# Decay attention and gated convolution: pinning two engines instead of five to the written order of steps

## The chip, the cores and the metric

The kernel runs on one core of a Trainium2 chip. The core has five engines that run side by side: TensorE (PE in the profile; its weight loads are a row of their own, PEld), VectorE (DVE), ScalarE (ACT), GpSimd (POOL) and SyncE (SP). Each engine takes the instructions of its own queue in order, and semaphores hold an instruction back until what it needs from another engine is there. SP does no arithmetic here; it only issues transfers, and so does POOL for some of them. Sixteen DMA engines move the data.

The metric is device time in microseconds, median of several runs. Lower is better.

## What is computed

All arrays are float32. For each of 4 x 8 heads (768 steps, 48 channels) a state decays by a complex factor and takes in the outer product of key and value; the query reads its real part. The heads are then laid side by side (384 channels), and a gated convolution with two projections follows.

```python
for t in range(S):
    ar, ai = (a_re_n[:, :, t, :, None], a_im_n[:, :, t, :, None])   # a, with its magnitude held under 0.999
    new_re = ar * S_re - ai * S_im
    new_im = ar * S_im + ai * S_re
    kv = np.einsum('bhd,bhe->bhde', k[:, :, t], v[:, :, t])
    S_re, S_im = (new_re + kv, new_im)
    y[:, :, t] = np.einsum('bhd,bhde->bhe', q[:, :, t], S_re)
...
x = y.transpose(0, 2, 1, 3).reshape(B, S, H * D)
gate = 1.0 / (1.0 + np.exp(-gate_pre))      # gate_pre: causal convolution of x, 5 taps per channel
val = x @ w_val
out = (gate * val) @ w_out
```

## The kernel before

The 32 heads are cut into ten units (line 76): two of two heads, six of four, two of two. A unit goes through these stages.

- **Loads.** `load` (line 109) brings `ar`, `ai`, `k` and `q` of a unit into one of six slots of the pool `ld` (tag "in"), each array by two transfers on SP (line 114). `load_v` (line 125) brings the values into a pool of three slots (line 132). A slot is free again when the last instruction that reads it is done.
- **Preparation.** `prep_x`, `prep_r`, `prep_a`, `prep_s` and `prep_e` (lines 269 to 367) turn the decay into logarithm and angle, sum both over time (ACT and DVE in turns, with the small matrix products of `offset` on PE), and give cosine, sine and two exponentials. The first step of a unit is the logarithm of `ar` on ACT (line 278); the product with `ai` on DVE (line 284) follows, then the square on ACT (line 289).
- **Scaling.** `prep_b` (line 369) multiplies keys and queries in (line 379, then line 382 into `kx`, of which there is one slot, and into `trig`). `kx` is written to a tensor in device memory, `kd`, by two transfers on SP (line 392).
- **Reading back.** `load_kn` (line 402) reads `kd` back, laid out by chunks of 128 steps, into one of three slots `kn`, for half a unit at a time. The first instruction of a slot is a small memset on POOL (line 407), then come three transfers on SP (line 413: one for the first half of the heads, two for the second, whose rows are swapped in halves).
- **Attention.** `transpose` (line 416) turns `kx` and the scaled queries by PE, and ACT copies them out (lines 430 and 431). For every chunk of a unit (60 in all) PE makes scores (lines 457, 458), DVE masks them into `sm` (line 464), PE makes the output from `sm` and from the state so far (lines 477, 480), ACT copies it (line 481), and PE and ACT carry the state on (lines 494 to 497).
- **Collecting.** `collect` (line 499) moves the attention's output into `xT`, channels on partitions, by transfers on POOL (line 509); `xT`'s first columns are zeroed by a memset on POOL (line 503).
- **Convolution and projection.** `conv` (line 515) is one multiplication (line 518) and four multiply-adds (line 521) on DVE for each group of channels. `gate` (line 527) is the sigmoid on ACT. `project` (line 531) makes the two matrix products on PE (line 255, tiles `pv` and `po`), the product with the gate on DVE (line 542), and the copy on ACT (line 576). The result leaves by transfers on POOL (line 813).
- **Weights.** `load_weights` (line 212) brings the weights in and converts them by short DVE and ACT instructions (lines 186 to 208).

What sets the order: `ORDER` (line 22) is a string with one letter per step, written out by hand, and the loop at line 850 takes it letter by letter. Capital `L`, `V` and `N` are the loads of lines 109, 125 and 402, `D` is `collect`, `O` an output transfer; `X x R r A a S E B` are the preparation, `T` is `transpose`, `s k t y` are scores, mask, state and output of a chunk, `C`, `G` and `M` convolution, gate and projection, `W` the weights. Between two steps the program checks (lines 605 to 834) that a step isn't written before what it builds on; these checks decide when a letter may stand, they are no waits of the chip.

The program text is then handed to a scheduler, which puts the instructions of each engine into a queue. It goes through the program in a timeline of its own: an engine that is idle there takes, of its instructions whose inputs and whose slot are ready, the one that was written first. Slots are given out in the same pass: an instruction that opens a tile takes whichever slot of its pool is free then. After that each queue is fixed, and the chip executes it in that order.

Before, the lines 855 to 865 take this freedom away. They go through all instructions and tie each one of an engine named in `IN_ORDER` to the one before it on the same engine. The tie is used for ordering alone; it makes no wait on the chip.

```python
before = {}
for ins in nc.cur_bb.bb.instructions:
    if ins.engine not in IN_ORDER:
        continue
    if ins.engine in before:
        tc.add_manual_dep(
            ins, before[ins.engine].name,
            mybir.DependencyInfo(mybir.DependencyClass.NoSync, mybir.DependencyReason.DATA),
            reason="the order that the steps are written in",
        )
    before[ins.engine] = ins
```

Of the kernel before, what the change touches and what calls it, by code (L numbers as in the profile page):

```python
# [32 lines left out]
    "MDMOOMMMMMOCCCCCCGMMMMMMMMOOMMO"  # L33
)
IN_ORDER = (
    mybir.EngineType.PE, mybir.EngineType.Activation, mybir.EngineType.DVE, mybir.EngineType.SP, mybir.EngineType.Pool
)
TURN = 2.0 ** 24
RADIAN = 2.0 * PI / 2.0 ** 32 * (1.0 - 2.0 ** -22)
# [962 lines left out]
```

## Time and profile before

| what | value |
| --- | --- |
| median of 3 runs | 351.83 us (351.12 to 354.74) |
| the profiled execution, whole | 351.17 us |
| its span, first to last instruction | 349.4 us |
| mean granted TensorE clock | 0.924 |
| ACT table loads (line 104), 31 of them | 39.8 us busy |
| moved by DMA | 53.31 MB, mean 153 GB/s |

The table's times are read in this way. The span is what the trace covers; the execution is 1.8 us longer than it. Busy time says how long an engine worked, and the rest of its span is waiting: the view of the waits lists, for each engine, which instruction waited, for what, how long in total, how often, and the longest single case. A row "SPq" there is the queue of the engine that issues transfers: while its head waits, everything behind it in the queue waits too. The timeline lists instructions with start and length; what stands in brackets at the end of a row is the idle time just before it and what ended that.

### The profile page before, as it was taken

The page shows a single profiled execution, that of the slowest core. Times are in us where ns is not written, and L with a number is a line of the kernel's source. Part 1 is how long each engine was busy: PE and PEld are TensorE (multiplying, and loading weights), DVE is VectorE, ACT ScalarE, POOL GpSimd, SP SyncE. Part 2 cuts the span into 40 slices and gives each one's busy share as a digit, 9 for nine tenths or more (in the row PEclk, how much of TensorE's full clock was granted, in tenths as well). Part 3 has the DMA queues.
Part 4 walks back from the last instruction along what each step waited for, and adds up shares of the span by engine and source line. Part 5 has one row for each costly group of instructions (what it writes and reads, how often), then busy time and mean ns, then how long its engine had stood idle before and what let it go on. Part 6 is the DMA issues. An engine that isn't in the chain of part 4 may idle for free.

```text
span 349.4 us, 8122 instructions
## 1 busy us (share of the span) xinstructions
PE 269.5 (77%) x3234; PEld 210.8 (60%) x3234; DVE 257.9 (74%) x341; ACT 245.7 (70%) x455; POOL 60.1 (17%) x148
## 2 busy tenths in 40 slices
PE   0033757668977999996669999979989999999960
PEld 0023646538866777576458787668779666766530
DVE  4799869995959999929297899577769956476400
ACT  5758789999657899987357989956996457553110
POOL 3000001111023032020212022200342031240210
PEclk9999887956989999999968999996999999999995
DMA  7993576768697851595969403768950441530220
GB/s 203 316 224 112 140 231 182 108 207 221 172 239 200 167 169 48 193 272 170 258 127 208 108 33 102 218 176 259 191 139 26 124 105 46 154 93 2 85 68 7
DMA packets 87804, 53.31 MB, mean 153 GB/s; under 512 B 36432, under 2 KB 84816, under 8 KB 87760
## 3 DMA queue, kind: packets, MB, share of 16 engines
q1 hardware_dynamic: 83664, 43.28, 48.8%
q0 software_dynamic: 4096, 9.44, 9.1%
q8 instruction: 27, 0.44, 0.5%
q14 instruction: 17, 0.14, 0.1%
HBM read 33.83 MB, written 14.16 MB: 137 GB/s over the span
## 4 chain that ended last, share of the span: by engine, by line
DMA 24%; DVE 19%; PE 18%; ACT 16%; issue 9%; SPq 8%; POOL 2%; POOLq 0%; DVEq 0%; ACTq 0%
DMA kn<-kd 14%; SPq L114 4%; ACT L104 4%; PE pt L430 3%; PE pv L255 3%; PE po L255 3%; ACT kq L431 3%; DVE sm L464 3%; DVE z L521 2%; DMA kd<-kx 2%; DVE kx L382 2%; DVE main L379 2%; DMA raw<-in_moe_w_val_dram 2%; SPq L413 2%; PE sc_ps L457 2%
## 5 line engine op out<-in xcount | busy, mean ns | idle before, releaser
L509 POOL DMA_DIRECT2D xT<-y_sb x80 | 40.8, 516 | 156.3 <-ACT y_sb L481 120.8
L431 ACT COPY kq<-pt 96x384 f32<-96x384 f32 x128 | 51.8, 508 | 4.4 <-PE pt L430 4.2
L521 DVE SCALAR_TENSOR_TENSOR z<-xT,cw_sb,z 128x768 f32<-128x768 f32 (+1 forms) x60 | 51.4, 856 | 1.7
L480 PE MATMUL y_ps<-sm,v_in 128*48 128x128 f32 x384 | 44.0, 294 | 10.2 <-DVE sm L464 10.2
L255 PE MATMUL po<-wo_sb,z 128*64 128x384 f32 x288 | 51.2, 488 | 0.0
L255 PE MATMUL pv<-xT,wv_sb 128*64 128x384 f32 x288 | 49.8, 486 | 0.0
L464 DVE TENSOR_TENSOR sm<-sc_ps,mask 128x512 f32<-128x512 f32 (+1 forms) x60 | 34.5, 578 | 15.9 <-PE sc_ps L458 11.8
L430 PE MATMUL pt<-ident,kx 128*96 128x128 f32 x192 | 37.9, 314 | 9.8 <-DVE kx L382 9.5
L457 PE MATMUL sc_ps<-kq 96*64 96x128 f32 x384 | 43.2, 286 | 1.7 <-DVE sm L464 1.7
L477 PE MATMUL y_ps<-kq,S_sb 96*48 96x128 f32 x320 | 38.5, 300 | 7.3 <-ACT y_sb L481 5.1
L458 PE MATMUL sc_ps<-kq 96*64 96x64 f32 x384 | 43.3, 229 | 0.0
L458 PEld LDWEIGHTS sc_ps<-kq 96*64 96x64 f32 x384 | 40.1, 143 | 2.0
L104 ACT ACT_TABLE_LOAD x31 | 39.8, 1283 | 1.3 <-PEq L986 0.8
L430 PE MATMUL pt<-ident,trig 128*96 128x128 f32 x192 | 36.7, 306 | 4.7 <-DVE trig L382 2.8
L457 PEld LDWEIGHTS sc_ps<-kq 96*64 96x64 f32 x384 | 33.6, 145 | 4.6 <-DVE sm L464 2.1
L255 PEld LDWEIGHTS pv<-xT,wv_sb 128*64 128x64 f32 x288 | 25.8, 137 | 16.1
L494 PE MATMUL S_ps<-v_in,kn 128*64 128x48 f32 x320 | 30.0, 233 | 7.2 <-ACT S_sb L497 5.1
L480 PEld LDWEIGHTS y_ps<-sm,v_in 128*48 128x48 f32 x384 | 28.6, 133 | 11.2 <-DVE sm L464 11.2
L481 ACT COPY y_sb<-y_ps 112x256 f32<-112x256 f32 (+1 forms) x60 | 19.5, 324 | 21.9 <-PE y_ps L480 21.6
L255 PEld LDWEIGHTS po<-wo_sb,z 128*64 128x64 f32 x288 | 24.6, 136 | 15.4 <-DVE z L542 1.5
L430 PEld LDWEIGHTS pt<-ident,kx 128*96 128x96 f32 x192 | 24.1, 144 | 14.4 <-issue 11.9
L477 PEld LDWEIGHTS y_ps<-kq,S_sb 96*48 96x48 f32 x320 | 22.6, 132 | 15.6 <-ACT y_sb L481 8.1
(84 smaller groups left out, 487.6 us busy)
## 6 DMA issues: line engine op xcount, KB each, us to landing
kd<-kx SPq DMA_DIRECT2D x12, 576.0 KB, 4.4
out_dram<-ot POOLq DMA_DIRECT2D x24, 192.0 KB, 2.5
ar_in<-in_a_re_dram SPq DMA_DIRECT2D x12, 288.0 KB, 4.5
ai_in<-in_a_im_dram SPq DMA_DIRECT2D x12, 288.0 KB, 5.2
k_in<-in_k_dram SPq DMA_DIRECT2D x12, 288.0 KB, 4.4
q_in<-in_q_dram SPq DMA_DIRECT2D x12, 288.0 KB, 4.4
xT<-y_sb POOLq DMA_DIRECT2D x48, 72.0 KB, 3.2
v_in<-in_v_dram SPq DMA_DIRECT2D x16, 144.0 KB, 5.1
```

What stands on the lines that cost most here:

```text
L104: nc.scalar.preload_act_table_set(name)
L255: nc.tensor.matmul(out[c:c + 64], lhsT[:, c:c + 64], rhs, **kw)
L430: nc.tensor.transpose(pt[:C2, j, :], src[:, j, f, h, :], ident)
L431: nc.scalar.copy(tj[:, s, f], pt[:C2].rearrange("c j p -> c p j"))
L457: nc.tensor.matmul(sc[lo:lo + half, h, :], k[:, :half], q, start=True, stop=True)
L458: nc.tensor.matmul(sc[hi:hi + half, h, half:], k[:, half:], q[:, half:], start=True, stop=True)
L464: nc.vector.tensor_tensor(out=two(sm), in0=two(sc[:, :g]), in1=mask[:, :, None, :].to_broadcast([C, 2, g // 2, C]), op=ALU.mult)
L477: nc.tensor.matmul(o, self.S_sb[n - 1][:, h * D:(h + 1) * D], self.part(1, h, n), start=True, stop=False)
L480: nc.tensor.matmul(o, vt[:, h, n], sm[:, h, :], start=(n == 0), stop=True)
L494: nc.tensor.matmul(S_all[:64, cols], kn[:, c0:c0 + 64], vt[:, h, n], **at_h)
L509: XQ.dma_start(out=xTs[b][c0 % P:c0 % P + c2 - c0, c0 // P, EXT + hf * HS:EXT + (hf + 1) * HS], in_=self.y[hf][r0:r0 + c2 - c0, h // 2],)
L521: nc.vector.scalar_tensor_tensor(out=z, in0=xT[:, c, EXT + t0 - t:EXT + t0 - t + n], scalar=cw_sb[:, TAPS - 1 - t, c:c + 1], in1=z, op0=AL ...
```

## The change

`IN_ORDER` names TensorE and ScalarE alone. The ties of lines 855 to 865 are made for these two as before; VectorE, SyncE and GpSimd get none, so that the scheduler orders their queues. The string of steps, the instructions themselves, the pools and their slots stay as they are.

```diff
@@ -33,7 +33,7 @@
     "MDMOOMMMMMOCCCCCCGMMMMMMMMOOMMO"
 )
 IN_ORDER = (
-    mybir.EngineType.PE, mybir.EngineType.Activation, mybir.EngineType.DVE, mybir.EngineType.SP, mybir.EngineType.Pool
+    mybir.EngineType.PE, mybir.EngineType.Activation
 )
 TURN = 2.0 ** 24
 RADIAN = 2.0 * PI / 2.0 ** 32 * (1.0 - 2.0 ** -22)
```

## The prediction

> **What bounds the kernel now.** I read the page's busy times first, then the waits of each engine, then the timeline of SP's queue against those of DVE and ACT.
>
> ```profile
> span 349.4 us, 8122 instructions
> PE 269.5 (77%) x3234; PEld 210.8 (60%) x3234; DVE 257.9 (74%) x341; ACT 245.7 (70%) x455; POOL 60.1 (17%) x148
> ```
>
> No engine is full. Three of them are near 250 us, so the span is made of work on PE, DVE and ACT and of stalls in which one holds up the others. The waits say what the stalls are.
>
> ```profile
> DVE main L284 <- DMA ai_in<-in_a_im_dram: 21.4, 5, 6.3
> DVE sm L464 <- PE sc_ps L458: 11.8, 6, 4.0
> DVE z L518 <- DMA xT<-y_sb: 8.2, 2, 5.0
> DVE sm L464 <- PE y_ps L480: 4.1, 3, 3.5
> ACT main L278 <- DMA ar_in<-in_a_re_dram: 13.1, 6, 4.5
> ACT tmp L289 <- DVE main L284: 8.2, 3, 6.0
> PE y_ps L480 <- DVE sm L464: 10.2, 6, 4.9
> PE pt L430 <- DVE kx L382: 9.5, 1, 9.5
> ```
>
> The largest wait of DVE is for the load of `ai`, and ACT's for a transfer is the load of `ar`. These loads are late because SP's queue is held up, which its own waits show:
>
> ```profile
> SPq L413 <- DMA kn<-kd: 70.3, 20, 6.9
> SPq L392 <- DVE kx L382: 44.0, 3, 23.6
> ```
>
> Each of the 20 reads of `kn` issues one transfer and then holds the queue until it has landed, 3.5 us on average; and a write of `kd` stands at the head of the queue until DVE has made `kx`. Loads behind them wait, although nothing they need is missing. Here is SP's queue, with the start of each entry:
>
> ```profile
> 122.16 1.00 SPq L114 DMA_DIRECT2D ar_in<-in_a_re_dram  x2
> 140.85 1.23 SPq L392 DMA_DIRECT2D kd<-kx  x2
> ...
> 148.63 1.22 SPq L114 DMA_DIRECT2D ai_in<-in_a_im_dram  x2
> ...
> 165.20 2.72 SPq L114 DMA_DIRECT2D ai_in<-in_a_im_dram  x2
> ...
> 191.75 1.03 SPq L114 DMA_DIRECT2D ar_in<-in_a_re_dram  x2
> ...
> 224.18 1.10 SPq L114 DMA_DIRECT2D ai_in<-in_a_im_dram  x2
> ...
> 233.22 0.92 SPq L114 DMA_DIRECT2D ar_in<-in_a_re_dram  x2
> ```
>
> and here DVE, with the idle time before an instruction in brackets:
>
> ```profile
> 109.32 1.35 DVE L284 TENSOR_TENSOR main<-tmp,ai_in 128x1152 f32<-128x1152 f32 x1
> ...
> 154.62 1.36 DVE L284 TENSOR_TENSOR main<-tmp,ai_in 128x1152 f32<-128x1152 f32 x1 [6.34 <-DMA ai_in<-in_a_im_dram]
> ...
> 174.28 1.36 DVE L284 TENSOR_TENSOR main<-tmp,ai_in 128x1152 f32<-128x1152 f32 x1 [6.02 <-DMA ai_in<-in_a_im_dram]
> 175.56 0.69 DVE L464 TENSOR_TENSOR sm<-sc_ps,mask 128x512 f32<-128x512 f32 x1
> ...
> 212.48 1.35 DVE L379 TENSOR_TENSOR main<-main,k_in 128x1152 f32<-128x1152 f32 x1
> ...
> 229.42 0.76 DVE L284 TENSOR_TENSOR main<-tmp,ai_in 128x576 f32<-128x576 f32 x1 [5.87 <-DMA ai_in<-in_a_im_dram]
> ```
>
> In the first of these stalls SP did nothing from 123.2 to 140.85 but wait for `kx`, with the load of unit 6's `ai` behind it.
>
> **What the change does to SP.** A load needs a free slot and nothing else. The row at 191.75 is the first load of unit 8, made while `k` of unit 6 (read at 212.48) still held its slot, so any free slot serves. Counting the loads of units 0 to 9 in their order against six slots, `ai` of a unit finds a slot once `ai` of the unit before and `k` and `q` of three units before are read. Unit 6's could go when 109.32 + 1.35 = 110.7 is past, and it went at 148.63; unit 7's could go at 156.0 (154.62 + 1.36) and went at 165.20; unit 8's could go at 175.6 (174.28 + 1.36) and went at 224.18. A load takes about 5 us:
>
> ```profile
> ai_in<-in_a_im_dram SPq DMA_DIRECT2D x12, 288.0 KB, 5.2
> ```
>
> so each would be there before DVE comes for it (148.3, 168.3 and 223.5, the starts less the idle times). A scheduler that issues what is ready will put these loads into the gaps of the `kn` reads, and these waits go. SP's other steps (values, `kd`, `kn`, 60 transfers of line 413 and 20 of line 392) are only passed by loads; what they lose is an issue of 0.6 us here and there, and the second and third transfers of a `kn` read wait for the first to land anyway.
>
> **What of it counts.** An idle DVE costs time only where another engine stands with it. In the last of the five rows below PE worked half of its time and ACT a third: DVE waits for `ai` of unit 7, `sm` of 175.56 stands behind it, PE waits 4.9 us for that `sm`, ACT waits 5.96.
>
> ```profile
> 221.70 0.67 ACT L278 ACTIVATE main<-ar_in 128x576 f32<-128x576 f32 x1
> 175.68 1.16 ACT L289 ACTIVATE tmp<-main 128x1152 f32<-128x1152 f32 x1 [5.96 <-DVE main L284]
> 236.59 0.68 ACT L278 ACTIVATE main<-ar_in 128x576 f32<-128x576 f32 x1 [4.53 <-DMA ar_in<-in_a_re_dram]
> 230.00:240.00 10.00, 7.20 (x98) 6.43 (x96) 9.91 (x10) 4.07 (x11) 0.00 (x0) 0.75 0.74 219
> 170.00:180.00 10.00, 5.12 (x33) 3.76 (x29) 5.68 (x6) 3.33 (x6) 0.51 (x2) 0.68 0.68 168
> ```
>
> I take 4.9 us for this stall, the least of the three waits. For the stall at 229 and 236 I take ACT's 4.5: unit 9's `ar` could go once unit 8's logarithm has read its own (221.70 + 0.67 = 222.4; by the count above `k` and `q` of unit 6 are read by then too), and went at 233.22; DVE was full just then (9.91 of 10) because 5.87 us of waiting had pushed its work there. The stall at 154 reached ACT with 1.7 (8.2 less 6.0 leaves 2.2 for two cases, and 0.6 of it lies in the next rows). In the early part ACT waits
>
> ```profile
> ACT main L278 <- DMA ar_in<-in_a_re_dram: 3.0, 2, 2.1
> ACT main L278 <- DMA ar_in<-in_a_re_dram: 1.6, 1, 1.6
> ACT tmp L289 <- DVE main L284: 0.6, 1, 0.6
> ACT main L278 <- DMA ar_in<-in_a_re_dram: 3.4, 1, 3.4
> ```
>
> (the first row from 0 to 30, the next two from 30 to 60, the last from 60 to 100). The first 3.0 are the kernel's start and stay; the others are 5.6 us. DVE is nearly full there, so I count half, 2.8. Together 4.9 + 4.5 + 1.7 + 2.8 = 13.9 us. The bounds: nothing, if PE is late next everywhere; and 21.4, DVE's whole wait.
>
> The granted clock of the 170 to 180 row is 0.68. The Trainium skill (page "TensorE: Matmul & The Clock Gate", Part 1) says that an idle window of about 3.4 us puts TensorE's clock to half until it has been busy for as long again; the row agrees in kind, and by that rule each of three stalls gone would give some 1.7 us more, an estimate, for a sum near 336.
>
> **What the change does to DVE.** Its 341 instructions stay; where the scheduler sees DVE idle, it takes a later step early. A step in progress can't be broken off, so an urgent `sm` that comes meanwhile waits for the rest of it. That can happen where DVE now idles ahead of `sm`, 6 + 3 times by the waits; half a mean DVE instruction is 257.9 / 341 / 2 = 0.38 us, together 3.4 us lost. Against it stand PE's 9.5 us for one `kx` and the 5.3 us for `sm` not counted yet (10.2 less 4.9): between 14.8 gained and, by the convolution rival below, some 20 lost. I take the 3.4 lost, since most of DVE's time is full and the order hardly free there.
>
> **What it does to POOL.** Its memsets, 80 collecting transfers and 24 output transfers may pass each other.
>
> ```profile
> POOL xT L509 <- ACT y_sb L481: 120.8, 16, 18.3
> POOL kn L407 <- PE S_ps L494: 2.0, 1, 2.0
> ```
>
> POOL mostly waits for ACT, whose order stays, so I cost this at nothing. The cover is the 17% load; if it is gone, a collecting step of five transfers waits behind an output transfer, half a microsecond each.
>
> **Sum.** The profiled execution is 351.17 us, its span 349.4; the median 351.83 is 0.7 above. 351.17 - 13.9 + 3.4 = 340.7, so **341 us**, 3% faster.
>
> **Rivals.**
>
> *The convolution's heads block DVE (slower).* The queue is fixed by the scheduler's own estimate of when data comes, and the chip can't pass a head that is not ready. The Trainium skill (page "PSUM — Partial Sum Buffer", section "Engine vs sequencer instructions") calls the queues of VectorE and GpSimd strict FIFO; the `sm` of 175.56 behind its late neighbour agrees. The place is line 518, 15 starts, each after transfers of `xT`. Pulled forward while DVE seems idle, such a start stands at the head until its transfer lands:
>
> ```profile
> xT<-y_sb POOLq DMA_DIRECT2D x48, 72.0 KB, 3.2
> ```
>
> Now two starts wait, 8.2 us, 4.1 each, with masks and preparation behind. It decides from three more starts on (10.5 / 4.1 = 2.6). With five it gives 340.7 + 5 x 4.1 = 361 us. For it: two such waits exist even in the written order. Against it: a start that is ready in the written order is ready at the same place still.
>
> *Earlier loads delay the reads of kn (no change).* DMA engines are busy 0.68 to 0.74 of the time in the two windows above. The slowest `kn` transfers show what a full system does; a queue wait was 3.5 us on average and 6.9 at the most. If 3 of the 20 reads come 3.4 us later with PE waiting, 10 us are lost, and the time is 351. Against it: the bytes stay the same, and loads would leave a busy place as often as they enter one.
>
> *PE is late next, or the scheduler's order is the written one (no change).* In its own timeline the stalls may not exist, and then the tie removes nothing: 351. Against it: the queue of SP holds loads back for reasons that any timeline sees.
>
> **Chances.** The forecast 0.49; DVE's reordering gaining as well (329 to 335) 0.05; no change, by the two rivals together, 0.16; slower 0.30. A measurement of this kernel tells about 1% from no change, so faster by more than that 0.54, within 0.16, slower 0.30. The forecast's own range is 334 to 347. The whole range starts at 330, with DVE's 14.8 partly got beside the loads, and ends at 362, with five blocked starts; 0.2 lies outside, most of it above.
>
> **What would show it.** SP's queue has loads of line 114 inside the groups of line 413, and unit 6's `ai` goes before 125. The waits of line 284 for `ai` and of line 278 for `ar` fall under 5 us each (3.0 of the latter are the start of the kernel). ACT's wait at line 289 is near 0. Wrong is the prediction if DVE's waits for `xT` at line 518 or PE's for `sm` grow by 10 us, if SP's wait for `kx` holds up `kn` instead, or if the waits for `ai` stay.

## The result

The changed kernel takes 341.53 us (median; 337.84 to 341.84) beside 351.48 us before (350.68 to 354.74). The ratio is 0.968, with a 95% interval of 0.959 to 0.977: faster by some 10 us. A second measurement beside the experiments below gave 0.974 (0.967 to 0.982). A time in us is here the median of all executions, while ratios and intervals leave out the slow ones (one of 679.82 us among the four with the convolution alone free, for example), so where the two differ the ratio is the better measure.

The page of the changed kernel begins like this; the busy times are nearly those of before, and the span is 9.3 us shorter.

```profile
span 340.1 us, 8134 instructions
PE 263.1 (77%) x3234; PEld 202.9 (60%) x3234; DVE 253.3 (74%) x341; ACT 246.4 (72%) x455; POOL 60.7 (18%) x148
```

The waits of the changed kernel, engine by engine (total, times, longest):

```profile
DVE main L284 <- DMA ai_in<-in_a_im_dram: 2.7, 1, 2.7
DVE z L518 <- DMA xT<-y_sb: 27.2, 8, 6.4
ACT main L278 <- DMA ar_in<-in_a_re_dram: 3.1, 2, 1.8
ACT tmp L289 <- DVE main L284: 0.2, 1, 0.2
ACT z L529 <- DVE z L521: 13.4, 6, 4.7
PE y_ps L480 <- DVE sm L464: 4.8, 5, 1.9
SPq L114 <- DVE main L379: 60.1, 6, 27.3
SPq L413 <- DMA kn<-kd: 34.4, 17, 4.4
```

The waits for late loads are nearly gone: line 284 waited 21.4 us for `ai` and waits 2.7, line 278 waited 13.1 for `ar` and waits the 3 of the start, line 289 waited 8.2 and waits 0.2. Two waits have grown. Line 518, where a convolution starts, waited 8.2 us for `xT` and now waits 27.2; and ACT at the sigmoid of line 529 waited 4.8 us for the convolution

```profile
ACT z L529 <- DVE z L521: 4.8, 3, 2.2
```

(this row is of the kernel before) and now waits 13.4. PE's wait for the masks of line 464 fell from 10.2 to 4.8. SP's queue is held less by the `kn` reads (34.4 after 70.3) and is now held by loads that wait for a free slot.

The timeline of SP's queue in the changed kernel shows how the loads get through: a read of `kn` issues its first transfer, and loads are issued while that lands.

```profile
94.75 0.43 SPq L413 DMA_DIRECT2D kn<-kd  x1
95.22 1.04 SPq L114 DMA_DIRECT2D k_in<-in_k_dram  x2
100.76 1.28 SPq L413 DMA_DIRECT2D kn<-kd  x2
...
115.05 1.01 SPq L114 DMA_DIRECT2D ai_in<-in_a_im_dram  x2
```

The last row is unit 6's `ai`, issued at 148.63 before. The stall of unit 7 is gone as well. Its line 284, at 174.28 before, now starts at 164.48, so the work of the old stretch from 170 to 180 (PE busy 5.12 of 10 us, granted clock 0.68) lies some ten us earlier now. These rows give the window, its length, the busy time of PE, PEld, DVE, ACT and POOL with the number of instructions, then granted clock, DMA share and GB/s:

```profile
160.00:170.00 10.00, 8.64 (x167) 7.35 (x163) 9.28 (x10) 7.92 (x14) 3.27 (x8) 1.00 1.03 302
170.00:180.00 10.00, 10.00 (x147) 8.95 (x145) 1.74 (x2) 9.35 (x23) 3.07 (x6) 1.00 0.98 234
180.00:190.00 10.00, 6.15 (x45) 3.76 (x42) 9.49 (x12) 7.29 (x8) 0.00 (x0) 1.00 0.23 34
```

In the first two PE works most or all of the time at a clock of 1.00. In the third it has a new stall, which comes back below.

So the result alone leaves two readings. Either the earlier loads are worth about 10 us and DVE's new order is nearly neutral (theory A, the prediction's sum), or the loads are worth much more and the convolution starts eat part of it (theory A2). A rival, B, has DVE gain by filling its gaps.

### The profile page after: what moved, and what is told of

Its sections match the earlier page's. It is cut to its first block, busy times and chain, and to the rows that moved or that the text cites. A ratio compares the mean times of both kernels' runs of the same rounds, so it can differ in the third digit from the quotient of the medians.

```text
span 340.1 us, 8134 instructions
## 1 busy us (share of the span) xinstructions
PE 263.1 (77%) x3234; PEld 202.9 (60%) x3234; DVE 253.3 (74%) x341; ACT 246.4 (72%) x455; POOL 60.7 (18%) x148
## 4 chain that ended last, share of the span: by engine, by line
PE 31%; DVE 28%; issue 12%; ACT 10%; DMA 9%; POOL 4%; SPq 2%; DVEq 0%; POOLq 0%; ACTq 0%
DVE z L521 7%; PE po L255 7%; DMA xT<-y_sb 6%; PE pt L430 6%; DVE kx L382 3%; PE sc_ps L457 3%; POOL xT L509 3%; PE y_ps L480 3%; PE pv L255 3%; DVE sm L464 3%; PE y_ps L477 3%; DMA raw<-in_moe_w_val_dram 3%; PE off L255 2%; DVE main L249 2%; ACT L104 2%
## 5 line engine op out<-in xcount | busy, mean ns | idle before, releaser
L509 POOL DMA_DIRECT2D xT<-y_sb x80 | 41.7, 527 | 86.7 <-ACT y_sb L481 78.5
L480 PE MATMUL y_ps<-sm,v_in 128*48 128x128 f32 x384 | 41.9, 284 | 4.8 <-DVE sm L464 4.8
L477 PE MATMUL y_ps<-kq,S_sb 96*48 96x128 f32 x320 | 36.0, 285 | 10.1 <-ACT y_sb L481 6.8
L430 PE MATMUL pt<-ident,kx 128*96 128x128 f32 x192 | 35.5, 298 | 8.8 <-DVE kx L382 8.7
L464 DVE TENSOR_TENSOR sm<-sc_ps,mask 128x512 f32<-128x512 f32 (+1 forms) x60 | 34.4, 578 | 10.4 <-PE y_ps L480 5.5
L458 PEld LDWEIGHTS sc_ps<-kq 96*64 96x64 f32 x384 | 39.1, 142 | 1.9 <-issue 0.3
L430 PE MATMUL pt<-ident,trig 128*96 128x128 f32 x192 | 35.1, 295 | 4.1 <-DVE trig L382 3.9
L457 PEld LDWEIGHTS sc_ps<-kq 96*64 96x64 f32 x384 | 33.4, 143 | 5.7 <-DVE sm L464 3.0
L477 PEld LDWEIGHTS y_ps<-kq,S_sb 96*48 96x48 f32 x320 | 21.0, 124 | 18.6 <-ACT y_sb L481 10.1
L255 PE MATMUL off<-main,dturn 128*64 128x192 f32 (+1 forms) x80 | 9.5, 365 | 28.7 <-DVE main L249 28.4
L480 PEld LDWEIGHTS y_ps<-sm,v_in 128*48 128x48 f32 x384 | 27.2, 128 | 5.8 <-DVE sm L464 5.6
L430 PEld LDWEIGHTS pt<-ident,kx 128*96 128x96 f32 x192 | 22.6, 136 | 13.0 <-issue 10.9
```

The source lines that it names most:

```text
L255: nc.tensor.matmul(out[c:c + 64], lhsT[:, c:c + 64], rhs, **kw)
L430: nc.tensor.transpose(pt[:C2, j, :], src[:, j, f, h, :], ident)
L457: nc.tensor.matmul(sc[lo:lo + half, h, :], k[:, :half], q, start=True, stop=True)
L458: nc.tensor.matmul(sc[hi:hi + half, h, half:], k[:, half:], q[:, half:], start=True, stop=True)
L464: nc.vector.tensor_tensor(out=two(sm), in0=two(sc[:, :g]), in1=mask[:, :, None, :].to_broadcast([C, 2, g // 2, C]), op=ALU.mult)
L477: nc.tensor.matmul(o, self.S_sb[n - 1][:, h * D:(h + 1) * D], self.part(1, h, n), start=True, stop=False)
```

## The experiments

### Which queue does it

The ties are made for other sets of engines:

```diff
-    mybir.EngineType.PE, mybir.EngineType.Activation
+    PE, Activation, DVE, Pool        (SyncE alone free)
+    PE, Activation, SP, Pool         (VectorE alone free)
+    PE, Activation, DVE, SP          (GpSimd alone free)
+    PE, Activation, DVE              (SyncE and GpSimd free)
```

SyncE alone free:

> SyncE alone is left to the scheduler; VectorE and GpSimd are tied as before. Theory A (the gain is the earlier loads, and VectorE's free order neither wins nor loses much): 338 to 344 us, the wait of line 284 for ai under 3 us in all, the wait of line 518 for xT near the 8 us of before. Theory A2 (the loads win more, and VectorE's free order gives some of it back through the convolution starts that wait 27 us in the changed kernel): 332 to 338. Theory B (the gain is VectorE filling its own gaps): 348 to 352, since the loads alone free a VectorE that then waits for something else.

VectorE alone free:

> VectorE alone is left to the scheduler; SyncE and GpSimd are tied as before. Theory A: 350 to 354, since the loads are as late as before and line 284 still waits about 21 us for ai. Theory A2: 353 to 360, the convolution starts wait more and nothing pays for it. Theory B: 340 to 345.

GpSimd alone free:

> GpSimd alone is left to the scheduler. Theories A and B: 350 to 353, no change, since GpSimd waits for ScalarE, whose order stays. Theory C (the memsets of kn and xT that now pass waiting transfers let the reads of kn start earlier): 344 to 348.

SyncE and GpSimd free, measured together with the runs on the convolution below:

> SyncE and GpSimd are free, VectorE is tied: the changed kernel without its VectorE part. Theory A2 (loads win some 20 us, VectorE's free order gives 10 back): 329 to 333 us, as SyncE alone. Rival F (GpSimd's free order is what costs in the changed kernel, since it makes reads of kn pass outputs and collecting transfers): 338 to 342.

| queues left to the scheduler | us | ratio to before (95% interval) |
| --- | --- | --- |
| SyncE | 330.75 | 0.939 (0.933 to 0.946) |
| VectorE | 355.95 | 1.015 (1.010 to 1.019) |
| GpSimd | 352.82 | 1.005 (1.001 to 1.009) |
| SyncE, GpSimd | 332.56 | 0.943 (0.936 to 0.951) |
| all three: the change | 341.53 | 0.968 (0.959 to 0.977) |

Theory A2 holds, and A and B fall. SyncE's freedom alone is worth 20 us, twice what the change shows and somewhat more than A2 had said (332 to 338 us). VectorE's is a loss: 5 us by itself, as A2 said, and 9 us beside a free SyncE and GpSimd (332.56 against 341.53; the intervals do not meet). GpSimd's costs some half a per cent alone and nothing that can be told beside SyncE (the first and fourth row overlap), so F and C fall. The kernel with SyncE alone free beats both kernels. SyncE and VectorE free with GpSimd tied was not run.

The waits of DVE, first with SyncE alone free, then with VectorE alone free, show where the two differ:

```profile
DVE z L518 <- DMA xT<-y_sb: 9.5, 3, 5.1
DVE main L284 <- DMA ai_in<-in_a_im_dram: 2.3, 2, 1.8
```

```profile
DVE main L284 <- DMA ai_in<-in_a_im_dram: 8.8, 5, 2.9
DVE z L518 <- DMA xT<-y_sb: 26.6, 8, 5.4
```

VectorE alone does shorten its own wait for `ai`, from 21.4 to 8.8, with the order of SyncE's queue unchanged, since it does other steps meanwhile; the kernel is slower all the same. The idle time moved to line 518.

How the lead builds up is read from the start of line 284 in five units (us; columns: before, SyncE alone free, the change):

| unit | before | SyncE free | change |
| --- | --- | --- | --- |
| 3 | 52.41 | 50.70 | 52.61 |
| 5 | 109.32 | 103.17 | 102.15 |
| 6 | 154.62 | 143.28 | 145.73 |
| 8 | 229.42 | 209.26 | 217.46 |
| 9 | 246.19 | 227.87 | 235.29 |

Up to unit 5, whose line 284 comes some 4 us after the first convolution start (97.89 in the changed kernel), the change is as good as SyncE alone. From there it falls back by 2.4 us at unit 6 and by 8.2 at unit 8. The second profiled execution of the change has unit 6 at 142.65, still 0.6 us ahead of SyncE alone, and unit 8 at 215.56, 6.3 us behind; so what both show is a loss between units 6 and 8.

### Which of SyncE's steps

Here all five engines are tied, but `load` marks its transfers, and the loop leaves the marked ones out of the chain; in a second kernel `load_v` marks its own as well.

```diff
-        if ins.engine not in IN_ORDER:
+        if ins.engine not in IN_ORDER or ins.name in loose:
             continue
```

> All five engines are tied as before, but the loads of ar, ai, k and q (line 114) are left out of SyncE's chain of ties; the values, kd, kn and the weights keep their written order. Theory A: the same as with all of SyncE free, within 2 us. Rival D (what counts on SyncE is that kd and kn pass waiting transfers, or that the values come earlier): less than half of the gain of all of SyncE free.

> All five engines are tied as before, but the loads of ar, ai, k and q and those of the values (lines 114 and 132) are left out of SyncE's chain; kd, kn and the weights keep their written order. If the 6 us that SyncE as a whole won beyond the four loads are the values that come earlier (TensorE waited 6.4 us for them with the four loads free): 329 to 333 us, and that wait is gone. If they are kd and kn passing what waits: 335 to 338.

The four loads alone give 336.83 us, 0.957 (0.947 to 0.966), some 14 of the 20 us. That is more than half, against rival D, but not within 2 us of the whole, as theory A had said: the interval lies above that of the whole SyncE. With the four loads free PE had a wait that it had little of before,

```profile
PE S_ps L494 <- DMA v_in<-in_v_dram: 6.4, 2, 4.4
```

(2.0 us in two cases before). With the values free too this wait is gone, and the time is 333.38 us, 0.945 (0.939 to 0.952). That is just past the 333 expected if the values are the rest and well short of 335, and its interval meets both neighbours, so the size of their share stays open. The order of SyncE's queue narrows it down. With SyncE free no transfer of `kd` or `kn` stands ahead of a transfer of another kind that was written before it, so the gain can't come from `kd` and `kn` passing what waits. What does stand earlier, beside the four loads, are values (ahead of `kd` and `kn`) and the five small transfers of the convolution's weights (line 223, from 64.82 us on before, from 22.38 on with SyncE free). No run frees these weights alone.

The other way round, in the changed kernel the loads of line 114 are held: none may go ahead of a SyncE step written before it.

```diff
+        if ins.engine == mybir.EngineType.SP:
+            for x in since if ins.name in held else ():
+                tc.add_manual_dep(ins, x, ...)
+            since = [ins.name] if ins.name in held else since + [ins.name]
```

> The changed kernel, but no load of ar, ai, k or q may be placed ahead of a SyncE step written before it; the other SyncE steps, VectorE and GpSimd stay free. If the earlier loads carry the change's gain: 350 to 356 us, as with VectorE alone free, with line 284's wait for ai back over 8 us. Rival D (kd, kn and the values, which stay free, carry a good part): 341 to 347.

The time is 347.04 us, 0.986 (0.978 to 0.994): just past D's range and short of the other, and line 284's wait for `ai` came back to 6.8 us, not over 8. Holding the loads takes more than half of the change's gain (4 of 10 us are left), as the loads' theory says in kind; but the other SyncE steps, left free, still bring the kernel 9 us below the 355.95 us with VectorE alone free, as D says. Here too it is values and weights that stand ahead; `kd` and `kn` pass only a few transfers (two pairs of `kd` with `kn`, six of `kn` with loads or values). So the loads are worth 14 us where they alone are freed from the written order, and 5.5 us (347.04 less 341.53) where everything else is free already. That either kind of step relieves the same queue would explain the difference; no run shows it.

### What VectorE's order costs

First the starts of the convolution: in the changed kernel none may be placed ahead of a VectorE step that was written before it (`starts` holds the instructions of line 518).

```diff
+        if ins.engine == mybir.EngineType.DVE:
+            for x in since if ins.name in starts else ():
+                tc.add_manual_dep(ins, x, ...)
+            since = [ins.name] if ins.name in starts else since + [ins.name]
```

> The changed kernel, but no convolution start (line 518) may be placed ahead of a VectorE step that was written before it; all other VectorE steps stay free. Theory A2: 330 to 334, the wait of line 518 for xT down from 27 us to under 12. Rival E (VectorE's reordering costs in its preparation and mask steps, whatever the convolution does): 338 to 342, with the wait of line 518 down all the same.

Then the opposite: SyncE and GpSimd free, VectorE tied but for lines 518 and 521, which are left out of the chain as the loads were above.

> SyncE and GpSimd are free, VectorE is tied except for the convolution steps (lines 518 and 521), which the scheduler may pull forward. Theory A2: 337 to 342, with the wait of line 518 near 27 us: the convolution alone brings the whole cost. Rival E: 329 to 333.

And the changed kernel beside them:

> The changed kernel once more beside these, on the same chip. All theories: 338 to 343 us.

| kernel | us | ratio (interval) | line 518 for xT, us | line 529, us |
| --- | --- | --- | --- | --- |
| VectorE tied | 332.56 | 0.943 (0.936 to 0.951) | 13.2 | 6.9 |
| convolution alone free | 335.35 | 0.953 (0.945 to 0.961) | 20.8 | 8.8 |
| VectorE free, starts held | 337.98 | 0.960 (0.952 to 0.968) | 12.6 | 13.8 |
| VectorE free | 341.95 | 0.974 (0.967 to 0.982) | 21.4 | 12.6 |

The waits are read from one execution each. In the last two rows another 4.3 us before a start of line 518 are put down to PE's scores (line 458); the same start waited 4.4 us for `xT` in the first profile of the change, which had 27.2 us in eight cases.

Neither expectation came true. Holding the starts gives about 4 of the 9 us, and freeing the convolution alone costs about 3, although eight starts wait there as they do in the change. Both steps are smaller than the intervals, which overlap with their neighbours'. Still, a waiting start is not a price by itself: a price of its whole wait would have made 7.6 us of the second step. Three timelines of DVE at the same place, unit 5's `kx`, show why. First the changed kernel:

```profile
147.00 1.35 DVE L379 TENSOR_TENSOR main<-main,k_in 128x1152 f32<-128x1152 f32 x1
151.05 0.62 DVE L518 TENSOR_SCALAR z<-xT,cw_sb 128x768 f32<-128x768 f32 x1 [2.70 <-DMA xT<-y_sb]
151.79 4.18 DVE L521 SCALAR_TENSOR_TENSOR z<-xT,cw_sb,z 128x768 f32<-128x768 f32 x4
155.88 2.55 DVE L382 TENSOR_TENSOR kx<-trig,main 128x2304 f32<-128x2304 f32 x1
```

then the one with the convolution alone free:

```profile
143.61 1.35 DVE L379 TENSOR_TENSOR main<-main,k_in 128x1152 f32<-128x1152 f32 x1
146.78 0.62 DVE L518 TENSOR_SCALAR z<-xT,cw_sb 128x768 f32<-128x768 f32 x1 [1.83 <-DMA xT<-y_sb]
147.52 3.12 DVE L521 SCALAR_TENSOR_TENSOR z<-xT,cw_sb,z 128x768 f32<-128x768 f32 x3
150.56 2.55 DVE L382 TENSOR_TENSOR kx<-trig,main 128x2304 f32<-128x2304 f32 x1
```

and the one with VectorE tied:

```profile
145.39 1.35 DVE L379 TENSOR_TENSOR main<-main,k_in 128x1152 f32<-128x1152 f32 x1
149.66 2.56 DVE L382 TENSOR_TENSOR kx<-trig,main 128x2304 f32<-128x2304 f32 x1 [2.93 <-PE pt L430]
```

In the last one DVE stands idle for 2.9 us here, because `kx` has one slot and PE is still reading it. The scheduler fills that gap with a convolution whose `xT` is not there yet, and `kx` starts 7.5 us after line 379 ends in the changed kernel, 5.6 us with the convolution alone free, 2.9 us with VectorE tied. By these rows a pulled start costs what it takes beyond the gap it fills. (In the second profile of the change it is 7.5 us again.)

How VectorE's delay reaches the span shows in PE's waits. PE idles for 77.0 us in the change (340.1 less 263.1) and for 67.5 with VectorE tied (330.7 less 263.2): that is the whole difference of the two spans. The longest stall that the change adds comes after a start that waited. First the change, DVE and PE, then PE with VectorE tied:

```profile
180.43 0.62 DVE L518 TENSOR_SCALAR z<-xT,cw_sb 128x768 f32<-128x768 f32 x1 [6.38 <-DMA xT<-y_sb]
189.89 1.21 PE L255 MATMUL off<-main,dturn 128*64 128x192 f32 x8 [3.85 <-DVE main L249]
```

```profile
183.91 0.87 PE L255 MATMUL off<-main,dturn 128*64 128x192 f32 x8 [1.60 <-DVE main L249]
```

The sums of line 249 for unit 7 stand behind the late convolution, and PE waits for them: 3.83 us also in the second profile of the change, 2.17 with the starts held, 0.51 with the convolution alone free.

The rest must lie in what the start does not show. ACT's wait at line 529 stays at 13.8 us with the starts held. The first such wait of the changed kernel, on DVE and then ACT:

```profile
116.30 0.95 DVE L249 TENSOR_TENSOR main<-main 128x768 f32<-128x768 f32 x1
117.17 1.01 DVE L521 SCALAR_TENSOR_TENSOR z<-xT,cw_sb,z 128x768 f32<-128x768 f32 x1
118.10 0.95 DVE L249 TENSOR_TENSOR main<-main 128x768 f32<-128x768 f32 x1
118.97 1.01 DVE L521 SCALAR_TENSOR_TENSOR z<-xT,cw_sb,z 128x768 f32<-128x768 f32 x1
```

```profile
120.01 0.84 ACT L529 ACTIVATE z<-z 128x768 f32<-128x768 f32 x1 [2.36 <-DVE z L521]
```

Two sums of the preparation (line 249) stand between the last multiply-adds, ahead of their written place. With VectorE tied both come after the convolution, and ACT does its three sigmoids in one piece:

```profile
115.97 2.49 ACT L529 ACTIVATE z<-z 128x768 f32<-128x768 f32 x3
```

ACT's order is pinned, so whatever stands behind the sigmoid waits. From this comes theory G, tested by two kernels: in one, no VectorE step written after a convolution step may be placed ahead of it; in the other, the convolution keeps its place both ways (`taps` holds the instructions of lines 518 and 521; the first kernel leaves out `since`).

```diff
+        if ins.engine == mybir.EngineType.DVE:
+            for x in last + (since if ins.name in taps else []):
+                tc.add_manual_dep(ins, x, ...)
+            since = [] if ins.name in taps else since + [ins.name]
+            if ins.name in taps:
+                last = [ins.name]
```

> The changed kernel, but no VectorE step written after a convolution step (lines 518 and 521) may be placed ahead of it; convolution starts may still be pulled forward. Theory G (besides the early starts, VectorE's free order costs because preparation and mask steps overtake the last multiply-adds, and ScalarE, whose order is pinned, stands at the sigmoid of line 529): ScalarE's wait at line 529 down from 13 us to about 7, and 335 to 338 us. Rival E (the loss lies among preparation, weights and mask steps themselves): the wait at line 529 falls, but the time stays at 339 to 342.

> The changed kernel with the convolution steps kept in place both ways: none is pulled ahead of a VectorE step written before it, and none is overtaken by one written after it. All other VectorE steps are free between them. Theory G: 331 to 335 us, within 2 of the kernel with VectorE tied. Rival E: 336 or more.

Not overtaken alone: 338.06 us, 0.957 (0.950 to 0.964), line 529's wait at 9.4 us where about 7 was expected. That is just past the end of what G said, and its interval overlaps one of the change's two, so alone it shows little. Kept in place both ways: 335.09 us, 0.951 (0.945 to 0.956). Its interval lies below both of the change's, and the time is 2.5 us above the kernel with VectorE tied, where G had said 2 at the most. Its two waits are back where they are with VectorE tied:

```profile
DVE z L518 <- DMA xT<-y_sb: 11.8, 4, 5.4
ACT z L529 <- DVE z L521: 7.1, 4, 2.2
```

Steps that keep their place also keep the other steps from swapping across them, so this kernel could have tied more than the convolution. The traces show that it did so only a little: among the pairs of other VectorE instructions, 332 stand the other way round than written in the change and still 280 here. Of pairs of a convolution step and another step the change has 150 reversed (101 with the convolution pulled ahead, 49 with it overtaken), and this kernel none.

So the placement of the convolution against the other VectorE steps, in both directions together, carries about 6.5 of the 9 us (341.53 less 335.09; 6 to 8 by the ratios of the change's two measurements). How this splits into the two directions is not shown, since with either alone the interval still overlaps at least one of the change's. The remaining 2.5 us are within the intervals and stay open; what is left of rival E would lie in them.

## Why the prediction was right, and where it was not

The total came out at 341 forecast and 341.53 measured, well inside the range and with the sign that the chances favoured. The total is better than its terms, and that it fits so closely is luck.

- **SyncE's queue.** The mechanism was right: the loads go into the gaps of the `kn` reads, unit 6's `ai` goes before 125, the waits at lines 284, 278 and 289 fall as said, and with SyncE alone free these waits fall just as far (2.3, 3.0 and 0.2 us). Its size was not. The term was 13.9 us and SyncE alone measured 20. The loads alone give 14, so the count of the stalls was close for them. What the sum left out is that the values and the convolution's weights also go earlier when SyncE is free. The prediction said that SP's other steps "are only passed by loads"; that held for `kd` and `kn`, and not for the values.
- **VectorE's order.** The term was 3.4 us lost, half an instruction at nine places. Measured are 9, the difference between VectorE tied and free beside a free SyncE and GpSimd. The failed step is "I take the 3.4 lost, since most of DVE's time is full and the order hardly free there": 247 of the 341 instructions stand at another place in VectorE's queue than written, and the loss does not show as `sm` behind a step in progress (PE's wait for `sm` at line 480 is 4.8 us in the change and 5.2 with VectorE tied); most of it came from the convolution's place.
- **The rival of the convolution's heads** was real. The text named a rise of DVE's wait for `xT` by 10 us as a sign that the prediction is wrong; it rose by 19, and the kernel was faster all the same, since the loads had gained more. Its price of 4.1 us for each start was too high: with the convolution alone free eight starts wait 20.8 us, 7.6 us more than with VectorE tied, and the time is only about 3 us longer. And it saw one direction, starts pulled forward, where steps that overtake the convolution's end count as well.
- **Delayed reads of kn** did not come: PE's wait for `kn` at line 495 was 5.8 us before and is 2.6 after:

```profile
PE S_ps L495 <- DMA kn<-kd: 2.6, 3, 1.1
```

- **GpSimd** was costed at nothing. Alone it measured 0.5% slower, beside SyncE nothing that can be told.
- **The clock.** With unit 7's stall gone the granted clock is 1.00 from 160 to 190, and PE's 3234 matmuls take 263.1 us where they took 269.5. After the new stall of 3.85 us, which ends at 189.89, the clock is 0.57 and 0.58 in the two stretches of 2 us from 190 to 194, and 1.00 again in the next. The Trainium skill's rule on idle windows (page "TensorE: Matmul & The Clock Gate", Part 1) agrees in kind with both. No run here separates what this is worth in time.

So two errors of about 6 us, in opposite directions, met in a sum that fits.

## What to carry to other kernels

A queue whose head waits for something slow is worth freeing for work that needs only a free slot: here loads without inputs brought most of the gain. A compute engine is another matter; here a step moved into a gap did harm where its own inputs were not there yet and it ended after the gap, and while the order of other engines is pinned, a step that overtakes may hold one of them. When a change lifts several restrictions at once, measure each alone: here no kernel measured better than the one that lifts one of the three.

## What was not expected

The scheduler's filling of VectorE's gaps made the kernel slower by itself (355.95 us, ratio 1.015, interval 1.010 to 1.019) although it took 12.6 us off the engine's longest wait. Loads issued as soon as a slot is free become the new head of SyncE's queue: they hold it 60.1 us in six cases, the longest 27.3, nearly as much as the `kn` reads did before (70.3), while DVE and ACT wait for loads of line 114 no more than the 2.7 and 3.1 us above.
